# Later four modulation rows read transposed by DMA, with one VectorE product and sum per 128 columns

## Chip, cores and metric

The kernel runs on one core of a Trainium2 chip. The metric is the device time of one execution in microseconds, lower is better; before the change the three runs gave 842.69, 842.85 and 844.57 us, median 842.85 us. One further execution was profiled; every time inside a trace below is of that execution and is counted from its first instruction.

## What is computed

One transformer layer with adaptive layer norm: a condition vector `c` makes six rows of 1024 numbers, which scale and shift the inputs of two blocks and gate their outputs. The first block is linear attention, the second a SwiGLU feed-forward. Matrices are bf16, 2048 tokens, width 1024, feed-forward width 3584.

```python
mod = (_silu(c) @ w_mod).reshape(1, 6, 1, -1)          # c (1, 1024), w_mod (1024, 6*1024)
sa, ca, ga, sb, cb, gb = (mod[:, i] for i in range(6))
h = _layernorm(x) * (1 + ca) + sa
q, k, v = split(h @ wqkv)                              # 32 heads of 32
pq, pk = phi(q), phi(k)                                # phi(t) = where(t > 0, t + 1, exp(t)) + 1e-6
kv, z = pk^T v, sum(pk)                                # per head
o = (pq kv) / (pq z + 1e-6)
x = x + ga * (o @ wo)
h = _layernorm(x) * (1 + cb) + sb
x = x + gb * ((silu(h @ w_gate) * (h @ w_up)) @ w_down)
```

The change concerns how four of the six rows, `ga`, `cb`, `sb` and `gb`, are made from `w_mod`. Rows `sb` and `cb` are needed with their 1024 numbers down the 128 partitions (eight columns of 128, tiles `sbT` and `cb1T`), because they are per-partition operands of a modulation; rows `ga` and `gb` are needed on every partition, 1024 numbers along it (`ga_bc`, `gb_bc`), because they scale the columns of `wo` and `w_down`.

## The kernel before

The tokens are four blocks of 512 (`sc` 0 to 3), each of four tiles of 128 (`st`). The width is eight chunks of 128 columns (`cc`), the contraction of every projection. A projection group is eight matmuls of 128x512, 1.73 us on TensorE.

The schedule is written out by hand. `add(label, fn)` builds a list of groups: V(0,0..7), then for each block KV(sc), Q(0,..) once, K(sc+1,0..7), V(sc+1,0..7), then Q(1..3), then GU(sc,0..27) (gate and up columns of the feed-forward) and D (the down projection). `put(label, fn)` hangs work behind a group. What is put goes into the in-order queues of the engines at that place, so the label fixes the order on each engine, and nothing else does. K(2,3) below is the group of block 2, number 3, of the K projection.

- `k_group` and `q_group` (L255, L269) leave their result in one of five PSUM banks in rotation (`nextbank`, L237). A K or Q result is taken out by one ScalarE exponential (L244) and two VectorE instructions (L245, L246); a V result by one ScalarE copy (L267). A bank is written again five groups later, so an evacuation may be late by a few groups before TensorE waits.
- `ln` (L223) normalizes a token tile: statistics on VectorE (L203 to L207), small steps and the normalization on GpSimd (L209 to L218), then a DMA transpose from the SP queue (L227) that lays the tile into `M4` with its columns down the partitions. Block 2 is normalized while K(1,..) runs, block 3 while K(2,..) runs. `modulate` (L231, eight VectorE instructions for each block, put at V(1,4), V(1,6) and V(2,4), V(2,6)) must be done before the first K group of that block reads `M4`.
- `nd_tr` (L473) and `o_tr` (L504) are DMA transposes from the ScalarE queue, used in Q(1..3) and in GU(0,2) to GU(0,24). `o_mm` (L485) is the output projection of one token tile, 16 matmuls, put into GU(0,..) too.
- `load_x` (L140), the weight loads (L516, L517), the loads of `w_mod` and of `wo` (L620) are issued from the SP queue in order.

The four late rows before the change: `load_late` (L299) loads half a row's columns, 1 MB, with `w_mod`'s rows down the partitions (eight rows on each partition, `j`). For `cb`, TensorE multiplies these with `silu(c)` as 64 matmuls of one column (`late_vec`, L328, at K(1,2) and K(1,6)). For `ga`, `sb` and `gb`, VectorE sums the eight rows of each partition with their factors, 512 columns at a time (`late_sum`, L305 and L307), and splits the sum into a bf16 part and a bf16 rest (`late_split`, L312, L313); a matmul with ones then adds over the partitions, spread over all of them for `ga` and `gb` (`late_bc`, L342, then a ScalarE copy L343) or as columns for `sb` (`late_cols`, L320). `ga` is used when `wo` is scaled (L637, eight VectorE instructions), `gb` when `w_down` is (L683).

Of the kernel before, what the change touches and what calls it, by code (L numbers as in the profile page):

```python
# [21 lines left out]
def kernel(  # L22
# [19 lines left out]
    DC = D // P  # L42
# [20 lines left out]
    wo_v = A_wo.rearrange("(c p) n -> p c n", p=P)  # L63
# [13 lines left out]
    bank = [psum.tile([P, NB], F32, name=f"bank{i}") for i in range(8)]  # L77
# [3 lines left out]
    M3 = const.tile([P, 16384], BF16, name="M3")  # L81
    M4 = const.tile([P, NSC, DC, SCW], BF16, name="M4")
    M5 = const.tile([P, 14336], BF16, name="M5")
    M6 = const.tile([P, 8192], BF16, name="M6")
    M7 = const.tile([P, 12288], BF16, name="M7")

    def view(region, off, shape, dtype=BF16):
        n = 1
        for s_ in shape:
            n *= s_  # L90
        w = n * (2 if dtype == F32 else 1)
        ap = region[:, off:off + w]
        if dtype == F32:
            ap = ap.bitcast(F32)
        if len(shape) == 2:
            ap = ap.rearrange("p (a b) -> p a b", a=shape[0])
        elif len(shape) == 3:
            ap = ap.rearrange("p (a b c) -> p a b c", a=shape[0], b=shape[1])
        return ap
# [5 lines left out]
    wd_lo = view(M12, 14336, [14, D])  # L105
    wme = view(M3, 0, [DC, 2 * D])
    pqT = view(M3, 0, [NSC, HG, SCW])
    wml = [view(M3, 4096 * (1 + i), [DC, NB]) for i in range(3)]
    wd_hi = view(M3, 0, [14, D])
    pk = view(M5, 0, [STC, D])  # L110
    v_c = view(M5, 4096, [STC, HG, VW])
# [6 lines left out]
    wo = view(M6, 0, [DC, D])  # L118
    x1rs = [view(M6, 2048 * i, [D], F32) for i in range(2)]
    obs = [view(M6, 4096 + 1024 * i, [D]) for i in range(2)]  # L120
    accA = view(M5, 8256, [D], F32)
    hlA = [view(M5, 10304 + 1024 * i, [2, NB]) for i in range(2)]
    accG = view(M3, 12288, [D], F32)
    hlG = view(M3, 14336, [2, NB])
    xs = [view(M7, 1024 * i, [D]) for i in range(6)]
    xns = [view(M7, 6144 + 1024 * i, [D]) for i in range(6)]
    wgs = [view(M7, 4096 * i, [DC, FBW]) for i in range(3)]
# [41 lines left out]
    ident = const.tile([P, P], BF16, name="ident")  # L169
# [8 lines left out]
    sbT = const.tile([P, DC], BF16, name="sbT")  # L178
    cb1T = const.tile([P, DC], BF16, name="cb1T")
    m1 = const.tile([P, 6, DC], BF16, name="m1")  # L180
    ga_bc = const.tile([P, D], BF16, name="ga_bc")
    gb_bc = const.tile([P, D], BF16, name="gb_bc")
    KVZ = const.tile([P, HG, KVW], BF16, name="KVZ")
    ones = const.tile([P, P], BF16, name="ones")
    nc.gpsimd.memset(ones[:], 1.0)
    scF = const.tile([P, DC], F32, name="scF")

    scT = const.tile([P, DC], BF16, name="scT")
    nc.scalar.activation(out=scT[:], in_=c_sb[:], func=ACT.Silu)
    nc.scalar.copy(out=scF[:], in_=scT[:])  # L190

    def warm(n):
        for _ in range(n):
# [100 lines left out]

    GA, SB, CB, GB = 2, 3, 4, 5

    def load_late(q, kb, slot):
        k0 = q * D + kb * NB
        nc.sync.dma_start(out=wml[slot], in_=wm_v[:, :, k0:k0 + NB])  # L299

    def late_sum(acc, kb, slot, js):
        dst = acc[:, kb * NB:(kb + 1) * NB]
        for j in js:
            if j == 0:
                nc.vector.tensor_scalar_mul(out=dst, in0=wml[slot][:, 0, :], scalar1=scF[:, 0:1])  # L305
            else:
                nc.vector.scalar_tensor_tensor(out=dst, in0=wml[slot][:, j, :], scalar=scF[:, j:j + 1], in1=dst,  # L307
                                         op0=ALU.mult, op1=ALU.add)

    def late_split(acc, kb, hl):  # L310
        src = acc[:, kb * NB:(kb + 1) * NB]
        nc.vector.tensor_copy(out=hl[:, 0, :], in_=src)  # L312
        nc.vector.tensor_tensor(out=hl[:, 1, :], in0=src, in1=hl[:, 0, :], op=ALU.subtract)  # L313

    def late_cols(q, kb, hl):
        o = 320 + 8 * q
        for ii in range(NB // P):
            col = o + kb * (NB // P) + ii
            for s_ in range(2):
                nc.tensor.matmul(bank[7][:, col:col + 1], lhsT=hl[:, s_, ii * P:(ii + 1) * P], rhs=ones[:, 0:1],  # L320
                                 start=False, stop=(s_ == 1), skip_group_check=True)

    def late_vec(q, kb, slot):
        o = 320 + 8 * q
        for ii in range(NB // P):
            col = o + kb * (NB // P) + ii
            for j in range(DC):
                nc.tensor.matmul(bank[7][:, col:col + 1], lhsT=wml[slot][:, j, ii * P:(ii + 1) * P],  # L328
                                 rhs=scT[:, j:j + 1], start=False, stop=(j == DC - 1), skip_group_check=True)

    def late_fin(q):
        mps = bank[7][:, 320 + 8 * q:328 + 8 * q]
        if q == SB:
            nc.vector.tensor_copy(out=sbT[:], in_=mps)
        else:
            nc.vector.tensor_copy(out=m1[:, q, :], in_=mps)
            nc.vector.tensor_scalar_add(out=cb1T[:], in0=m1[:, q, :], scalar1=1.0)

    def late_bc(kb, hl, dst):
        b = nextbank()  # L340
        for s_ in range(2):
            nc.tensor.matmul(b[:], lhsT=ones[:], rhs=hl[:, s_, :], start=(s_ == 0), stop=(s_ == 1))  # L342
        nc.scalar.copy(out=dst[:, kb * NB:(kb + 1) * NB], in_=b[:])  # L343


    def tr0(st):
# [101 lines left out]
    def put(label, *fns):  # L448
        after.setdefault(label, []).extend(fns)
# [156 lines left out]
    put(("V", 1, 7), lambda: [load_x(st) for st in range(12, 16)])  # L606


    def sums(acc, kb, slot, labels):
        for i, lab in enumerate(labels):  # L610
            put(lab, lambda i=i: late_sum(acc, kb, slot, (2 * i, 2 * i + 1)))

    put(("V", 0, 6), lambda: load_late(CB, 0, 0), lambda: load_late(CB, 1, 1), lambda: load_late(GA, 0, 2))
    put(("K", 1, 2), lambda: late_vec(CB, 0, 0), lambda: load_late(GA, 1, 0))
    put(("K", 1, 6), lambda: late_vec(CB, 1, 1), lambda: load_late(SB, 0, 1))
    put(("V", 1, 7), lambda: late_fin(CB))
    sums(accA, 0, 2, [("V", 1, k) for k in range(4)])
    put(("V", 1, 3), lambda: late_split(accA, 0, hlA[0]), lambda: load_late(SB, 1, 2))
    put(("K", 2, 2), lambda: late_bc(0, hlA[0], ga_bc))
    put(("K", 2, 3), lambda: nc.sync.dma_start(out=wo, in_=wo_v))  # L620
    sums(accA, 1, 0, [("V", 2, k) for k in range(4)])
    put(("V", 2, 3), lambda: late_split(accA, 1, hlA[1]))
    put(("K", 3, 0), lambda: late_bc(1, hlA[1], ga_bc))
    for kb in range(2):
        sums(accA, kb, 1 + kb, [("V", 3, 4 * kb + k) for k in range(4)])
    put(("V", 3, 4), lambda: late_split(accA, 0, hlA[0]))
    put(("KV", 3, 0), lambda: late_split(accA, 1, hlA[1]))
    put(("Q", 1, 2), lambda: late_cols(SB, 0, hlA[0]), lambda: late_cols(SB, 1, hlA[1]), lambda: late_fin(SB))
    put(("GU", 0, 18), lambda: load_late(GB, 0, 0), lambda: load_late(GB, 1, 1))
    gb_at = [("GU", 0, f) for f in range(21, FC)] + [("GU", 1, f) for f in range(8)]  # L630
    for kb in range(2):
        sums(accG, kb, kb, gb_at[5 * kb:5 * kb + 4])
        put(gb_at[5 * kb + 3], lambda kb=kb: late_split(accG, kb, hlG))
        put(gb_at[5 * kb + 5], lambda kb=kb: late_bc(kb, hlG, gb_bc))
    for cc in range(DC):
        put(("K", 3, 2 + cc) if cc < 6 else ("V", 3, cc - 6),
            lambda cc=cc: nc.vector.tensor_tensor(out=wo[:, cc, :], in0=wo[:, cc, :], in1=ga_bc[:], op=ALU.mult))  # L637


    put(("KV", 3, 1), kvz_build)  # L640
# [82 lines left out]
```

## Time and profile before

| | |
|---|---|
| median of three runs | 842.85 us |
| profiled execution, whole time | 842.25 us |
| its span, first to last instruction | 840.4 us |
| TensorE clock granted | 0.999 |
| one projection group (8 matmuls, TensorE) | 1.73 us |
| K(1,0) to K(1,7) start | 60.71 us |
| V(1,0) start | 76.12 us |
| K(2,0) start | 90.84 us |
| V(2,0) start | 106.00 us |
| K(3,0) start | 120.72 us |
| GU(0,18) start | 307.70 us |

The whole time is 1.85 us more than the span: what lies before the first and after the last instruction. A stage of the kernel is read from the chain of waits, which lists TensorE's groups by start; a stage's load on the other engines is read from the timeline of each engine in that stretch. A group's `idle before` names what the engine waited for last. Busy shares over the whole span hide that VectorE is nearly full from 66 to 92 us and from 97 to 122 us and lightly used after 370 us.

### The profile page before, as it was taken

What the parts mean: (1) busy time and instruction counts of PE and PEld (TensorE: products, weight loads), DVE (VectorE), ACT (ScalarE), POOL (GpSimd) and SP (SyncE); (2) the same over time, 40 slices, a digit from 0 to 9 for tenths busy, and PEclk for the clock granted to TensorE, in tenths of its full rate; (3) what the DMA queues carried; (4) which work ended last, traced back from release to release, by engine and by line L of the source; (5) the groups of instructions that cost most, each with busy time, mean ns of one, the idle gap of its engine ahead of it and who ended that gap; (6) DMA issues with size and microseconds to landing.
All of it is one profiled execution on the core that took longest, in us unless ns stands there. A gap on an engine that the chain in (4) does not pass through costs nothing.

```text
span 840.4 us, 10723 instructions
## 1 busy us (share of the span) xinstructions
PE 833.5 (99%) x4292; PEld 391.3 (47%) x4292; DVE 356.5 (42%) x668; ACT 145.1 (17%) x271; POOL 79.9 (10%) x143
## 2 busy tenths in 40 slices
PE   8999999999999999999999999999999999999998
PEld 4454444544444444444444444444444444444445
DVE  5768779988655656635341111111101211111111
ACT  4333333323211111111110001111000111100000
POOL 2124220022122323100000000000000000000000
PEclk9999999999999999999999999999999999999999
DMA  9985491056599899787874225555322555211210
GB/s 291 310 244 138 133 243 46 16 154 133 126 225 225 224 226 287 190 248 226 251 241 142 76 69 151 151 151 152 105 75 82 156 155 152 76 38 44 76 69 26
DMA packets 203905, 128.62 MB, mean 153 GB/s; under 512 B 50768, under 2 KB 190032, under 8 KB 203856
## 3 DMA queue, kind: packets, MB, share of 16 engines
q1 hardware_dynamic: 163008, 98.58, 41.1%
q10 hardware_dynamic: 38544, 20.98, 11.4%
q0 software_dynamic: 2304, 8.39, 2.6%
q8 instruction: 33, 0.54, 0.3%
q14 instruction: 16, 0.13, 0.1%
HBM read 103.81 MB, written 12.58 MB: 139 GB/s over the span
## 4 chain that ended last, share of the span: by engine, by line
PE 97%; SPq 1%; DMA 1%; issue 0%; DVE 0%
PE bank L553 23%; PE bank L534 23%; PE bank L528 23%; PE bank L272 7%; PE bank L485 7%; PE bank L264 7%; PE bank L249 6%; DMA M<-in_w_mod_dram 1%; PE bank L458 1%; PE bank L281 1%; SPq L148 1%; SPq L145 0%; PE bank L342 0%; SPq L140 0%; PE bank L328 0%; PE bank L364 0%
## 5 line engine op out<-in xcount | busy, mean ns | idle before, releaser
L534 PE MATMUL bank<-M,M 128*128 128x512 bf16 x896 | 211.7, 379 | 0.0
L528 PE MATMUL bank<-M,M 128*128 128x512 bf16 x896 | 211.6, 379 | 0.0
L536 DVE TENSOR_TENSOR M<-bank,e 128x512 bf16<-128x512 f32 x112 | 77.5, 692 | 248.5 <-PE bank L534 247.1
L553 PE MATMUL bank<-M,M 128*128 128x512 bf16 (+2 forms) x728 | 148.0, 363 | 0.0
L531 ACT ACTIVATE e<-bank 128x512 f32<-128x512 f32 x112 | 66.8, 597 | 436.3 <-PE bank L528 423.6
L553 PEld LDWEIGHTS <-M 128*128 128x128 bf16 x952 | 90.9, 98 | 103.0
L534 PEld LDWEIGHTS <-M 128*128 128x128 bf16 x896 | 87.7, 98 | 105.7
L528 PEld LDWEIGHTS <-M 128*128 128x128 bf16 x896 | 87.3, 98 | 103.9
L556 DVE TENSOR_TENSOR M<-bank,M 128x512 bf16<-128x512 f32 (+2 forms) x34 | 22.5, 661 | 169.9 <-PE bank L553 169.9
L249 PE MATMUL bank<-M,M 128*128 128x512 bf16 x256 | 57.9, 379 | 1.0 <-DVE M L231 0.6
L485 PE MATMUL bank<-M,M 128*128 128x512 bf16 x256 | 57.9, 379 | 0.0
L272 PE MATMUL bank<-M,M 128*128 128x512 bf16 x256 | 57.7, 379 | 0.0
L264 PE MATMUL bank<-M,M 128*128 128x512 bf16 x256 | 55.9, 379 | 0.0
L244 ACT ACTIVATE e<-bank 128x512 f32<-128x512 f32 x64 | 37.8, 598 | 100.5 <-PE bank L272 48.8
L553 PE MATMUL bank<-M 128*128 128x512 bf16 x224 | 51.0, 379 | 0.0
L246 DVE SCALAR_TENSOR_TENSOR M<-bank,e 128x512 bf16<-128x512 f32 x64 | 44.3, 692 | 3.9
L264 PEld LDWEIGHTS <-M 128*128 128x128 bf16 x256 | 25.0, 98 | 30.2
L485 PEld LDWEIGHTS <-M 128*128 128x128 bf16 x256 | 25.0, 98 | 29.7
L249 PEld LDWEIGHTS <-M 128*128 128x128 bf16 x256 | 24.2, 98 | 29.5 <-DVE M L231 2.1
L245 DVE TENSOR_SCALAR e<-e 128x512 f32<-128x512 f32 x64 | 27.7, 433 | 23.4 <-ACT e L244 23.4
L272 PEld LDWEIGHTS <-M 128*128 128x128 bf16 x256 | 24.5, 98 | 27.6
L487 DVE TENSOR_TENSOR M<-bank,M 128x512 f32<-128x512 f32 x32 | 22.0, 689 | 13.3 <-PE bank L485 13.1
(74 smaller groups left out, 362.4 us busy)
## 6 DMA issues: line engine op xcount, KB each, us to landing
M<-in_B_w_gate_dram SPq DMA_DIRECT2D x56, 512.0 KB, 3.9
M<-in_B_w_up_dram SPq DMA_DIRECT2D x56, 512.0 KB, 4.9
M<-in_w_mod_dram SPq DMA_DIRECT2D x8, 1024.0 KB, 8.7
x_scratch<-M POOLq DMA_DIRECT2D x16, 512.0 KB, 5.6
M<-x_scratch ACTq DMA_DIRECT2D x16, 512.0 KB, 3.4
M<-in_B_w_down_dram SPq DMA_DIRECT2D x6, 1024.0 KB, 7.9
M<-in_A_x_dram SPq DMA_DIRECT2D x16, 256.0 KB, 6.6
M<-in_w_mod_dram SPq DMA_DIRECT2D x8, 512.0 KB, 7.1
```

The lines of the kernel that those rows point to most:

```text
L244: nc.scalar.activation(out=e[:], in_=acc, func=ACT.Exp)
L245: nc.vector.tensor_scalar(out=e[:], in0=e[:], scalar1=1.0, scalar2=PHI_EPS, op0=ALU.min, op1=ALU.add)
L246: nc.vector.scalar_tensor_tensor(out=dst, in0=acc, scalar=0.0, in1=e[:], op0=ALU.max, op1=ALU.add)
L249: nc.tensor.matmul(acc[:], lhsT=M4[:, sc_, cc, t * P:(t + 1) * P], rhs=wk[:, cc, h * NB:(h + 1) * NB], start=(cc == 0), stop=(cc == DC - 1))
L264: nc.tensor.matmul(acc[:], lhsT=M4[:, sc_, cc, t * P:(t + 1) * P], rhs=wv[:, cc, h * NB:(h + 1) * NB], start=(cc == 0), stop=(cc == DC - 1))
L272: nc.tensor.matmul(acc[:], lhsT=wq[:, cc, qc * P:(qc + 1) * P], rhs=M4[:, sc_, cc, :], start=(cc == 0), stop=(cc == DC - 1))
L485: nc.tensor.matmul(acc[:], lhsT=oTs[st % 3][:, cc, :], rhs=wo[:, cc, hs], start=(cc == 0), stop=(cc == DC - 1))
L528: nc.tensor.matmul(g_ps[:], lhsT=wg_blk[:, cc, fs], rhs=M4[:, sc_, cc, :], start=(cc == 0), stop=(cc == DC - 1))
L531: nc.scalar.activation(out=sg[:], in_=g_ps[:], func=ACT.Silu)
L534: nc.tensor.matmul(u_ps[:], lhsT=wu_blk[:, cc, fs], rhs=M4[:, sc_, cc, :], start=(cc == 0), stop=(cc == DC - 1))
L536: nc.vector.tensor_tensor(out=gus[sc_][:, f, :], in0=u_ps[:], in1=sg[:], op=ALU.mult)
L553: nc.tensor.matmul(y_ps[:, 0:w], lhsT=gus[sc_][:, f, t * P:(t + 1) * P], rhs=wd(f)[:, c0:c1], start=(f == 0), stop=(f == FC - 1))
```

## The change

All four late rows are now made alike. A row's 1024x1024 piece of `w_mod` is read by eight DMA transposes of 128x1024 each (source in HBM), so that the columns of `w_mod` lie down the partitions and its 1024 rows along them (`rowT`). `silu(c)` is spread over all partitions once (`sc_bc`). For each 128 columns one VectorE instruction then multiplies 1024 elements with `sc_bc` and sums them into one number per partition (`colF`). That is already the column form that `cb` and `sb` need. For `ga` and `gb` the column is repeated 128 times along the partition (`spread` into `rep`) and eight TensorE transposes of 128 columns turn it into the spread row (`late_bc`). `late_vec`, `late_split` and `late_cols` are gone, `gb_bc` shares the storage of `ga_bc`, and `rowT[1]` lies where `wo` will be, so that the load of `wo` moves from K(2,3) to V(2,5) and the scaling of `wo` from K(3,2)..V(3,1) to K(3,0)..K(3,7).

```diff
-    wml = [view(M3, 4096 * (1 + i), [DC, NB]) for i in range(3)]
-    accA = view(M5, 8256, [D], F32)
-    hlA = [view(M5, 10304 + 1024 * i, [2, NB]) for i in range(2)]
-    accG = view(M3, 12288, [D], F32)
-    hlG = view(M3, 14336, [2, NB])
+    rowT = [view(M3, 4096, [DC, DC, P]), view(M6, 0, [DC, DC, P])]
+    prod = [view(M5, 8256, [D], F32), view(M3, 12288, [D], F32)]
...
-    gb_bc = const.tile([P, D], BF16, name="gb_bc")
+    gb_bc = ga_bc
...
+    rep = const.tile([P, DC, P], BF16, name="rep")
+    sc_bc = const.tile([P, D], BF16, name="sc_bc")
+    colF = const.tile([P, 6, DC], F32, name="colF")
...
+    def load_late(q, i, js):
         for j in js:
+            nc.sync.dma_start_transpose(out=rowT[i][:, j], in_=wm_v[:, j, q * D:(q + 1) * D])
+
+    def late_sum(q, i, pr, bs):
+        for b in bs:
+            nc.vector.tensor_tensor_reduce(out=prod[pr].rearrange("p (j k) -> p j k", j=DC), in0=rowT[i][:, :, b, :],
+                                           in1=sc_bc[:].rearrange("p (j k) -> p j k", j=DC), scale=1.0, scalar=0.0,
+                                           op0=ALU.mult, op1=ALU.add, accum_out=colF[:, q, b:b + 1])
+
+    def late_fin(q):
+        if q == SB:
+            nc.vector.tensor_copy(out=sbT[:], in_=colF[:, q, :])
+        else:
+            nc.vector.tensor_copy(out=m1[:, q, :], in_=colF[:, q, :])
+            if q == CB:
+                nc.vector.tensor_scalar_add(out=cb1T[:], in0=m1[:, q, :], scalar1=1.0)
             else:
+                spread(nc.vector, m1[:, q, :])
+
+    def spread(eng, col):
+        eng.tensor_copy(out=rep[:], in_=col.unsqueeze(2).to_broadcast([P, DC, P]))
+
+    def late_bc(dst):
+        tp = nextbank()[:].bitcast(BF16).rearrange("p (c s) -> p c s", c=DC)
+        for cc in range(DC):
+            nc.tensor.transpose(tp[:, cc, :], rep[:, cc, :], ident[:])
+        nc.scalar.copy(out=dst[:].rearrange("p (c s) -> p c s", c=DC), in_=tp)
...
-    put(("V", 0, 6), lambda: load_late(CB, 0, 0), lambda: load_late(CB, 1, 1), lambda: load_late(GA, 0, 2))
-    put(("K", 1, 2), lambda: late_vec(CB, 0, 0), lambda: load_late(GA, 1, 0))
-    put(("K", 1, 6), lambda: late_vec(CB, 1, 1), lambda: load_late(SB, 0, 1))
-    put(("V", 1, 7), lambda: late_fin(CB))
-    sums(accA, 0, 2, [("V", 1, k) for k in range(4)])
-    put(("V", 1, 3), lambda: late_split(accA, 0, hlA[0]), lambda: load_late(SB, 1, 2))
-    put(("K", 2, 2), lambda: late_bc(0, hlA[0], ga_bc))
-    put(("K", 2, 3), lambda: nc.sync.dma_start(out=wo, in_=wo_v))
-    sums(accA, 1, 0, [("V", 2, k) for k in range(4)])
-    put(("V", 2, 3), lambda: late_split(accA, 1, hlA[1]))
-    put(("K", 3, 0), lambda: late_bc(1, hlA[1], ga_bc))
...
+    put(("V", 0, 1), lambda: spread(nc.gpsimd, scT[:]))
+    put(("V", 0, 5), lambda: late_bc(sc_bc))
+
+    def put_late(q, i, loads, sums, pr=0):
+        n = DC // len(loads)
+        for k, lab in enumerate(loads):
+            put(lab, lambda k=k: load_late(q, i, range(n * k, n * (k + 1))))
+        for k, lab in enumerate(sums):
+            put(lab, lambda k=k: late_sum(q, i, pr, (2 * k, 2 * k + 1)))
+        put(sums[-1], lambda: late_fin(q))
+
+    put_late(GA, 0, [("V", 0, 7), ("Q", 0, 2)], [("V", 1, k) for k in range(4)])
+    put(("K", 2, 2), lambda: late_bc(ga_bc))
+    put_late(CB, 1, [("Q", 0, 4), ("Q", 0, 6)], [("V", 2, k) for k in range(4)])
+    put(("V", 2, 5), lambda: nc.sync.dma_start(out=wo, in_=wo_v))
+    put_late(SB, 0, [("V", 1, 4), ("V", 1, 5), ("V", 1, 6), ("V", 1, 7)], [("V", 3, k) for k in range(4)])
+    put_late(GB, 0, [("GU", 0, 18 + k) for k in range(4)], [("GU", 0, 23 + k) for k in range(4)], 1)
+    put(("GU", 1, 0), lambda: late_bc(gb_bc))
     for cc in range(DC):
-        put(("K", 3, 2 + cc) if cc < 6 else ("V", 3, cc - 6),
-            lambda cc=cc: nc.vector.tensor_tensor(out=wo[:, cc, :], in0=wo[:, cc, :], in1=ga_bc[:], op=ALU.mult))
+        put(("K", 3, cc), lambda cc=cc: nc.vector.tensor_tensor(out=wo[:, cc, :], in0=wo[:, cc, :], in1=ga_bc[:],
+                                                               op=ALU.mult))
```

In the built program of the changed kernel each product and sum is two VectorE instructions, the product over 1024 elements and a read of the accumulator (128x1), and each product waits for the accumulator read before it. A DMA transpose from the SP queue and one from the ScalarE queue wait for each other's landing wherever they are neighbours in the order.

More of the change, by code (lines that the diff above doesn't have):

```diff
@@ L181 @@
     ga_bc = const.tile([P, D], BF16, name="ga_bc")
-    gb_bc = const.tile([P, D], BF16, name="gb_bc")
+    gb_bc = ga_bc
     KVZ = const.tile([P, HG, KVW], BF16, name="KVZ")
-    ones = const.tile([P, P], BF16, name="ones")
-    nc.gpsimd.memset(ones[:], 1.0)
-    scF = const.tile([P, DC], F32, name="scF")
+    rep = const.tile([P, DC, P], BF16, name="rep")
+    sc_bc = const.tile([P, D], BF16, name="sc_bc")
+    colF = const.tile([P, 6, DC], F32, name="colF")
     scT = const.tile([P, DC], BF16, name="scT")
     nc.scalar.activation(out=scT[:], in_=c_sb[:], func=ACT.Silu)
-    nc.scalar.copy(out=scF[:], in_=scT[:])
     def warm(n):
@@ L295 @@
     GA, SB, CB, GB = 2, 3, 4, 5
[L297 to L302, printed above, removed]
-        for j in js:
-            if j == 0:
-                nc.vector.tensor_scalar_mul(out=dst, in0=wml[slot][:, 0, :], scalar1=scF[:, 0:1])
-            else:
-                nc.vector.scalar_tensor_tensor(out=dst, in0=wml[slot][:, j, :], scalar=scF[:, j:j + 1], in1=dst,
-                                         op0=ALU.mult, op1=ALU.add)
@@ L310, in late_split @@
[L310 to L343, printed above, removed]
+    def load_late(q, i, js):
+        for j in js:
+            nc.sync.dma_start_transpose(out=rowT[i][:, j], in_=wm_v[:, j, q * D:(q + 1) * D])
[4 more added lines that the diff above has]
+                                           op0=ALU.mult, op1=ALU.add, accum_out=colF[:, q, b:b + 1])
@@ L606 @@
     put(("V", 1, 7), lambda: [load_x(st) for st in range(12, 16)])
-    def sums(acc, kb, slot, labels):
-        for i, lab in enumerate(labels):
-            put(lab, lambda i=i: late_sum(acc, kb, slot, (2 * i, 2 * i + 1)))
-    put(("V", 0, 6), lambda: load_late(CB, 0, 0), lambda: load_late(CB, 1, 1), lambda: load_late(GA, 0, 2))
-    put(("K", 1, 2), lambda: late_vec(CB, 0, 0), lambda: load_late(GA, 1, 0))
-    put(("K", 1, 6), lambda: late_vec(CB, 1, 1), lambda: load_late(SB, 0, 1))
-    put(("V", 1, 7), lambda: late_fin(CB))
@@ L617 @@
-    sums(accA, 0, 2, [("V", 1, k) for k in range(4)])
-    put(("V", 1, 3), lambda: late_split(accA, 0, hlA[0]), lambda: load_late(SB, 1, 2))
-    put(("K", 2, 2), lambda: late_bc(0, hlA[0], ga_bc))
-    put(("K", 2, 3), lambda: nc.sync.dma_start(out=wo, in_=wo_v))
-    sums(accA, 1, 0, [("V", 2, k) for k in range(4)])
-    put(("V", 2, 3), lambda: late_split(accA, 1, hlA[1]))
-    put(("K", 3, 0), lambda: late_bc(1, hlA[1], ga_bc))
-    for kb in range(2):
-        sums(accA, kb, 1 + kb, [("V", 3, 4 * kb + k) for k in range(4)])
@@ L626 @@
[L626 to L634, printed above, removed]
+    put(("V", 0, 1), lambda: spread(nc.gpsimd, scT[:]))
```

## The prediction

> **What bounds the kernel now.** I read the page first, then the chain of waits, then VectorE's timeline around the starts of K(2,0) and K(3,0), and the SP and ScalarE queues in GU(0,16) to GU(0,24).
>
> ```profile
> PE 833.5 (99%) x4292; PEld 391.3 (47%) x4292; DVE 356.5 (42%) x668; ACT 145.1 (17%) x271; POOL 79.9 (10%) x143
> ...
> PE 97%; SPq 1%; DMA 1%; issue 0%; DVE 0%
> ...
> 65.89 0.78 PE bank L328 x32
> ...
> 73.59 0.78 PE bank L328 x32
> ...
> 96.93 0.43 PE bank L342 x2
> ...
> 156.68 0.38 PE bank L320 x16
> ```
>
> From 28 us on TensorE never waits: the chain is its groups end to end. So only two things change the time: instructions taken from or given to TensorE, and new waits on it. The four lower lines price the first.
>
> ```profile
> 79.75 0.15 DVE L207 TENSOR_SCALAR veps<-mv 128x1 f32<-128x1 f32 x1
> 79.82 0.48 DVE L305 TENSOR_SCALAR M<-M,scF 128x512 f32<-128x512 bf16 x1
> 80.33 6.30 DVE L307 SCALAR_TENSOR_TENSOR M<-M,scF,M 128x512 f32<-128x512 bf16 x7
> ...
> 87.73 2.67 DVE L231 TENSOR_SCALAR M<-M,ca1T,saT 128x512 bf16<-128x512 bf16 x8
> ...
> 110.50 0.15 DVE L207 TENSOR_SCALAR veps<-mv 128x1 f32<-128x1 f32 x1
> ...
> 118.86 2.67 DVE L231 TENSOR_SCALAR M<-M,ca1T,saT 128x512 bf16<-128x512 bf16 x8 [0.29 <-DMA M<-M]
> ```
>
> VectorE is full before K(2,0) and K(3,0). The modulation of block 2 ends at 90.40, K(2,0) starts at 90.84 and reads its eighth chunk 7 x 0.216 us later, at 92.3: 1.9 us to spare. For block 3 it is 121.5 against 122.2: 0.7 us. What makes VectorE later there makes TensorE later.
>
> ```profile
> 299.25 2.12 ACTq L473 DMA_TRANSPOSE M<-M  x1
> ...
> 302.10 3.59 ACTq L504 DMA_TRANSPOSE M<-M  x1
> 305.79 0.60 ACT L531 ACTIVATE e<-bank 128x512 f32<-128x512 f32 x1 [6.33 <-PE bank L528]
> ...
> 310.07 1.63 ACTq L473 DMA_TRANSPOSE M<-M  x1
> ...
> 312.50 3.73 ACTq L504 DMA_TRANSPOSE M<-M  x1
> 316.59 0.60 ACT L531 ACTIVATE e<-bank 128x512 f32<-128x512 f32 x1 [6.31 <-PE bank L528]
> ```
>
> In GU(0,..) ScalarE's queue carries transposes between the activations that free the banks. A transpose that waits holds up the activation behind it.
>
> [...]692 ns for L246, 512 elements[...]L307 repeats every 0.90 us in V1 beside GpSimd's normalization, every 0.78 us in V3 without[...]
>
> **TensorE's own work.** Removed: 2 x 0.78 (L328), four pairs of L342 at 0.43, and 0.38: 3.67 us. Added: 3 x 8 transposes. Short matmuls L281 run 16 in 0.91 us, 57 ns each, so eight cost 0.45 and all 1.36. Net -2.3 us, the whole possible gain, and about the 0.3% (2.5 us) below which no change can be told.
>
> **sc_bc at V(0,5).** GpSimd's spread stands behind the first normalization, which ends at 41.42. At L218's 1.19 us it ends at 42.6; TensorE finishes V(0,5) at 31.27 + 6 x 1.727 = 41.63. It waits 1.0 us (between 0 and 1.6: repeated input unknown). The next transposes of block 1 come 1.2 us later; the modulation at 53.8 hides that.
>
> **Stage V1.** One new sum: 1.22 for the product, and an accumulator read near the 0.15 us of a 128x1 instruction less overlap, with a wait for the result: 1.35 (bounds 1.2 and 1.5). Eight are 10.8, plus 0.7 to 0.85 beside GpSimd (the 7 x 0.12 of L307): 11.5 us. The old sums and split took 79.82 to 87.73, 7.9. Then `late_fin` adds 0.2 and the spread on VectorE, repeated input[...], 1.2. VectorE enters V1 at 79.8 + 1.0 + 0.45 - 0.2 (a gap of L328's that closes) = 81.1. Sums end 92.6, modulation runs 94.0 to 96.6, K(2,0) ends 96.9. Unhindered it would end at 92.57 + 1.45 - 1.56 = 92.46. **Loss 4.4 us** (2.5 to 5.5).
>
> **Stage V2.** Count from K(2,0)'s end T. VectorE's K2 work ended at T + 18.0 before (110.57 against 92.57). Now the loads of x tiles 12 to 15 stand on SP behind six of the eight `sb` transposes, which wait for the last `ga` sum (92.6). Six issues are 7.5 us, the load lands some 3.5 us later, at 104; VectorE wants it at T + 4.5 = 101.4, so it waits 2.5. K2 work ends at T + 20.5 = 117.4, the `cb` sums at 128.9, modulation at 132.0, K(3,0) at 132.3. TensorE would be there at T + 28.15 + 1.73 = 126.8. **Loss 5.5 us** (2 if the x load is in time, 10 if transposes from HBM are slower). Other stages let this pass: five banks cover K2.
>
> **wo.** Its load waits for the last `cb` sum (128.9) and lands 10.2 us on (as before), 139.7 with issue. VectorE stands at the first scaling until then, and K(3,1)'s bank is free at 141.4; TensorE wants it at 132.3 + 0.9 + 5 x 1.73 = 141.8. Hidden by 0.4; each us later costs one. Afterwards scaling and evacuation repeat every 1.73 us (129.64, 131.37 before), TensorE's pace. `sb` sums end near Q(1,0)'s evacuation as before: nothing.
>
> **GB in GU(0,18) to GU(1,1).** The order is: SP pair, `nd_tr(15)`, SP pair, `o_tr(12)`, SP pair, `o_tr(13)`, SP pair, `o_tr(14)`, each waiting for the landing before it. A transpose there landed 4.8 to 7.4 us after issue (at 288.4 and 299.25), against 3.1 in quiet stretches. With 6.1 for a pair and 4.8 for a single: 308.5, 314.6, 319.4, 325.5. ScalarE then stands at `o_tr(12)` until 325.5 with GU(0,19)'s activation behind it, done 327.6; the fifth bank group after it wanted to start at 323.2: 4.5 us. The last pair lands near 347, the sums (8 x 1.35 with evacuations between) and the spread end at 364, and `late_bc` at GU(1,0) wants it at 361: 3.5 us more. With 4.5 and 3.2 all of this is hidden; at 7 and 5 it is about 13. I take **7 us** (0 to 13).
>
> Sum: 1.45 - 1.56 + 4.4 + 5.5 - 1.2 (L342 and L320 less the last two spreads) + 7 = 15.6. On the profiled execution, 842.25 (span 840.4 and 1.85 around it), 857.8; the median shown is 0.6 higher, so **858.4**.
>
> **Rivals.**
> 1. Only VectorE's stages cost, the alternation of queues doesn't: landings of 3 us. For it: quiet stretches show 3.1. Against: those in GU(0,16) to GU(0,20) show 6 to 12. 858.4 - 7 = 851.4; with the x load in time, 848.
> 2. HBM-sourced transposes occupy the queue far longer. At 3 us each, sixteen last from 52 to 100 instead of 73, block 2's four transposes follow to 105, landing 108: V1 loses 14 rather than 4.4, V2 4 more, GB 10 more, 882. It decides from about 2 us each (block 2 late at 92). For it: pieces of 256 bytes from HBM appear nowhere in the trace of before. Against: L227's 1.25[...].
> 3. Not slower: the new sum is cheap. VectorE must start modulating by 89.5 to hold nothing up; from 81.1, less 1.4 for fin and spread, 7.0 us are left for eight: 0.88 each. If it took [...] (0.69 as L683, 1024 elements), with GB landing fast and the x load in time, only -2.3 + 1.0 remains: 841.5. Against: the output is f32, and L307, f32 out, takes 748 for 512.
>
> **How the numbers follow.** Forecast 0.52 (850 to 868); rival 1 0.24 (845 to 852); rival 2 0.15 (866 to 895); rival 3 0.09 (839.5 to 845.3). The range 846 to 870 holds the forecast, nearly all of rival 1 and the low end of rival 2, and leaves out about 0.2. Slower (over 845.4): 0.91. Same, most of rival 3: 0.06. Faster would need no wait at all: 0.03.
>
> **What would show it.** L299 products near 1.2 us with a short read after each; K(2,0)'s and K(3,0)'s matmuls waiting for VectorE L227 of the new file (modulation), about 4 us each; VectorE waiting for an x load near 101 us; ScalarE idle ahead of `o_tr(12)` for a w_mod transpose, and TensorE gaps near 330 and 370 us; SP's w_mod transposes 1.3 us apart. I am wrong if the sums take under 0.9 us, or if TensorE shows gaps elsewhere, above all in K3 (wo).

## The result, and the profile after it

The changed kernel took 861.95 us (median of five runs, 860.67 to 864.75) against 842.69 us for the kernel before (five runs, 842.46 to 844.57): a ratio of 1.0228, 95% interval 1.0206 to 1.0250, so 2.3% slower. The profiled execution took 861.95 us too; its span is 860.1 us, 19.7 us above the span of before. What follows explains these 19.7 us. One execution among all those below, the one of run 2 that was profiled (885.37 us), ran from start to end at a lower granted clock (0.946); it is left out of that run's time, and its trace is read only for which waits it holds. Line numbers are now those of the changed kernel: L299 is the new product and sum, L295 its DMA transposes, L227 the modulation, L245 the K groups, L314 and L319 the spread and its TensorE transposes, L462 the output projection, L505 and L511 gate and up, L508 their activation, L481 `o_tr`, L450 `nd_tr`, L600 the load of `wo`, L605 its scaling.

First the page's busy line and its chain, as before, then TensorE's own list of waits (what it stood for, us in total, times, longest; the lines left out are waits before V(0,0)).

```profile
PE 832.0 (97%) x4148; PEld 390.6 (45%) x4228; DVE 357.2 (42%) x676; ACT 145.4 (17%) x269; POOL 83.1 (10%) x143
...
PE 86%; DVE 7%; DMA 2%; SPq 2%; issue 1%; POOL 0%; ACT 0%; ACTq 0%; DVEq 0%; POOLq 0%
```

```profile
PE bank L245 <- DVE M L227: 7.7, 4, 4.2
PE bank L462 <- ACT e L508: 5.8, 1, 5.8
PE bank L245 <- DVE M L242: 1.7, 1, 1.7
...
PE bank L319 <- POOL rep L314: 0.8, 1, 0.8
```

VectorE is busy as long as before (357.2 against 356.5 us): the change has not given it more work, it has put the work elsewhere. The chain, 97% TensorE before, is 86% now. Four kinds of wait carry the loss: the modulations (L227) ahead of K(2,0) and K(3,0), ScalarE's activation (L508) in front of an output projection, a bank in K2 (L242), and GpSimd's spread.

Where each was lost is read by comparing when the same TensorE group starts in the two traces (TensorE's timeline, which counts some starts 0.1 to 0.2 us earlier than the chain that the table of before was read from; us):

| start of | before | changed | difference |
|---|---|---|---|
| V(0,0) | 31.10 | 31.56 | +0.46 |
| K(1,0) | 60.54 | 62.44 | +1.90 |
| V(1,0) | 75.96 | 76.25 | +0.29 |
| K(2,1) | 93.31 | 97.99 | +4.68 |
| V(2,0) | 105.83 | 112.40 | +6.57 |
| K(3,1) | 123.62 | 135.69 | +12.07 |
| GU(0,18) | 307.70 | 319.26 | +11.56 |
| GU(0,22) | 328.42 | 348.48 | +20.06 |
| GU(1,8) | 381.08 | 400.73 | +19.65 |
| first down group | 450.14 | 469.80 | +19.66 |

So, as differences of neighbouring lines, 4.4 us go in stage V1 with K(2,0), 1.9 in K2, 5.5 in V2 with K(3,0), 8.5 between GU(0,18) and GU(0,22). V0 adds 1.4 with the spread of `silu(c)`, and K1 gives 1.6 back (the matmuls of `late_vec` are gone). Between K(3,1) and GU(0,18) 0.5 us come back and behind GU(0,22) 0.4, mostly because the old matmuls L320 and L342 are gone there. From GU(1,8) on nothing changes.

VectorE's timeline ahead of K(2,0) (start, duration, what) is to be held against the one of before; the third product, at 84.30, is the only slow one of the eight.

```profile
81.76 1.22 DVE L299 CUSTOM_DVE_ANT_0 M<-M,sc_bc 128x1024 f32<-128x1024 bf16 x1 [0.26 <-issue]
82.91 0.08 DVE L299 DVE_READ_ACCUMULATOR2_ANT colF<- 128x1 f32 x1
...
84.30 2.10 DVE L299 CUSTOM_DVE_ANT_0 M<-M,sc_bc 128x1024 f32<-128x1024 bf16 x1
...
91.50 1.22 DVE L299 CUSTOM_DVE_ANT_0 M<-M,sc_bc 128x1024 f32<-128x1024 bf16 x1
...
92.97 0.69 DVE L314 COPY rep<-m 128x1024 bf16<-128x1024 bf16 x1
93.58 2.67 DVE L227 TENSOR_SCALAR M<-M,ca1T,saT 128x512 bf16<-128x512 bf16 x8
```

A product lasts 1.22 us, its read 0.08, and the next starts 1.27 after it. Eight, one of them slow, last from 81.76 to 92.73; the modulation that began at 87.73 before begins at 93.58. TensorE's timeline shows the consequence, here and one block later; the first two lines are of before, the others of the changed kernel:

```profile
90.68 1.89 PE L249 MATMUL bank<-M,M 128*128 128x512 bf16 x8
...
120.55 1.89 PE L249 MATMUL bank<-M,M 128*128 128x512 bf16 x8
```

```profile
94.05 3.20 PE L245 MATMUL bank<-M,M 128*128 128x512 bf16 x8 [2.91 <-DVE M L227]
97.08 1.07 PE L277 MATMUL bank<-M 128*128 128x129 bf16 x16
...
131.45 3.27 PE L245 MATMUL bank<-M,M 128*128 128x512 bf16 x8 [4.17 <-DVE M L227]
134.56 1.07 PE L277 MATMUL bank<-M 128*128 128x129 bf16 x16
```

From the start of these eight matmuls to the start of what follows it is 3.03 us here and 3.11 one block later, instead of 1.73. Two things slow them. They follow their chunks of the modulation, 0.33 us apart; where only that holds them the group takes 2.49 (K(3,0) in run 3 below, from 127.34 to 129.83; the K matmuls behind it go at 0.22 us each, as in a group of 1.73). The rest, 0.5 us, is the clock: 0.50 granted from 94 to 96 us, 0.66 over the 4 us from 94 on.

In K2 the queue of SP and VectorE (timeline) show the loads of x tiles 12 to 15 (L137) behind six `sb` transposes, which wait for the last `ga` sum, and VectorE waiting for the first of them (the first line is of before, where L140 is the same load):

```profile
87.25 2.95 SPq L140 DMA_DIRECT2D M<-in_A_x_dram  x4
```

```profile
92.76 8.91 SPq L295 DMA_TRANSPOSE M<-in_w_mod_dram  x6
101.73 1.99 SPq L137 DMA_DIRECT2D M<-in_A_x_dram  x4
```

```profile
105.98 1.29 DVE L199 BATCH_NORM_STATS2 stats<-M 128x6 f32<-128x512 bf16 x2 [4.21 <-DMA M<-in_A_x_dram]
...
119.58 1.23 DVE L299 CUSTOM_DVE_ANT_0 M<-M,sc_bc 128x1024 f32<-128x1024 bf16 x1
...
130.98 2.67 DVE L227 TENSOR_SCALAR M<-M,ca1T,saT 128x512 bf16<-128x512 bf16 x8
```

From 105.98 to the end of this modulation VectorE's timeline has no wait. So the start of K(3,0) is set by when the x load landed and by VectorE's work behind it. TensorE's wait of 1.7 us for a bank in K2 is a part of the same lateness: without it TensorE would have waited that much longer ahead of K(3,0).

And the feed-forward stage, timeline of all engines:

```profile
319.53 16.73 SPq L295 DMA_TRANSPOSE M<-in_w_mod_dram  x4
...
330.42 1.25 ACTq L450 DMA_TRANSPOSE M<-M  x1
...
333.07 1.89 PE L462 MATMUL bank<-M,M 128*128 128x512 bf16 x8
...
338.81 1.25 ACTq L481 DMA_TRANSPOSE M<-M  x1
340.16 0.60 ACT L508 ACTIVATE e<-bank 128x512 f32<-128x512 f32 x1 [18.32 <-DMA M<-in_B_w_gate_dram]
...
340.81 3.57 PE L462 MATMUL bank<-M,M 128*128 128x512 bf16 x8 [5.85 <-ACT e L508]
...
344.18 2.74 PE L505 MATMUL bank<-M,M 128*128 128x512 bf16 x8
...
346.76 1.89 PE L511 MATMUL bank<-M,M 128*128 128x512 bf16 x8
```

In the kernel before, the same output projection runs without a gap:

```profile
321.51 3.62 PE L485 MATMUL bank<-M,M 128*128 128x512 bf16 x16
```

The first pair of `gb` transposes is issued at 319.53 and 322.80 and lands 10.1 and 7.5 us later; `nd_tr(15)` starts at 330.42, when both are in; the second pair starts at 333.59, when that is in; `o_tr(12)` starts at 338.81, when the pair is in. The releaser that the profile names for the activation is a weight load; the two issued at 317.26 and 318.99 had landed after 3.7 and 5.6 us, so it wasn't that: the instruction ahead of it in ScalarE's queue is what held it. TensorE ran out of banks at 334.96 and stood 5.85 us. The eight matmuls after the wait then take 3.37 us to the start of the next group and the gate group behind them 2.58, instead of 1.73 each: in that stretch, 340.8 to 346.5 us, the granted clock is 0.55. So the wait cost 8.5 us, not 5.9. By the microsecond the granted clock is 0.50 in each from 340.8 to 345.8, and 1.00 from 346.7 on. The shorter wait of 2.91 us ahead of K(2,0) had 0.50 behind it too, for 2 us.

### The profile page after: what moved, and what is told of

It is laid out like the page before. It is cut to its first block, busy times and chain, and to the rows that moved or that the text cites. A ratio compares the mean times of both kernels' runs of the same rounds, so it can differ in the third digit from the quotient of the medians.

```text
span 860.1 us, 10559 instructions
## 1 busy us (share of the span) xinstructions
PE 832.0 (97%) x4148; PEld 390.6 (45%) x4228; DVE 357.2 (42%) x676; ACT 145.4 (17%) x269; POOL 83.1 (10%) x143
## 4 chain that ended last, share of the span: by engine, by line
PE 86%; DVE 7%; DMA 2%; SPq 2%; issue 1%; POOL 0%; ACT 0%; ACTq 0%; DVEq 0%; POOLq 0%
PE bank L530 22%; PE bank L505 22%; PE bank L511 22%; PE bank L462 6%; PE bank L268 6%; PE bank L245 3%; DVE M L299 2%; PE bank L260 2%; DVE M L242 2%; DVE stats L199 1%; DMA M<-in_A_x_dram 1%; DMA M<-in_w_mod_dram 1%; PE bank L435 1%; DVE e L241 1%; SPq L295 1%
## 5 line engine op out<-in xcount | busy, mean ns | idle before, releaser
L505 PE MATMUL bank<-M,M 128*128 128x512 bf16 x871 | 210.5, 380 | 1.3
L511 PE MATMUL bank<-M,M 128*128 128x512 bf16 x880 | 210.3, 379 | 0.9
L508 ACT ACTIVATE e<-bank 128x512 f32<-128x512 f32 x112 | 66.5, 597 | 446.3 <-PE bank L505 395.7
L511 PEld LDWEIGHTS <-M 128*128 128x128 bf16 x896 | 87.7, 98 | 105.7
L505 PEld LDWEIGHTS <-M 128*128 128x128 bf16 x896 | 87.5, 98 | 104.6 <-issue 1.7
L245 PE MATMUL bank<-M,M 128*128 128x512 bf16 x247 | 59.6, 392 | 10.4 <-DVE M L227 7.7
L462 PE MATMUL bank<-M,M 128*128 128x512 bf16 x254 | 59.6, 387 | 6.0 <-ACT e L508 5.8
L242 DVE SCALAR_TENSOR_TENSOR M<-bank,e 128x512 bf16<-128x512 f32 x64 | 44.3, 692 | 3.9
L245 PEld LDWEIGHTS <-M 128*128 128x128 bf16 x256 | 24.8, 99 | 41.3 <-DVE M L227 13.2
L462 PEld LDWEIGHTS <-M 128*128 128x128 bf16 x256 | 25.3, 99 | 36.7 <-issue 7.8
L299 DVE CUSTOM_DVE_ANT_0 M<-M,sc_bc 128x1024 f32<-128x1024 bf16 x32 | 40.9, 1278 | 1.1 <-issue 0.3
```

The lines of the kernel that those rows point to most:

```text
L242: nc.vector.scalar_tensor_tensor(out=dst, in0=acc, scalar=0.0, in1=e[:], op0=ALU.max, op1=ALU.add)
L245: nc.tensor.matmul(acc[:], lhsT=M4[:, sc_, cc, t * P:(t + 1) * P], rhs=wk[:, cc, h * NB:(h + 1) * NB], start=(cc == 0), stop=(cc == DC - 1))
L299: nc.vector.tensor_tensor_reduce(out=prod[pr].rearrange("p (j k) -> p j k", j=DC), in0=rowT[i][:, :, b, :], in1=sc_bc[:].rearrange("p (j k ...
L462: nc.tensor.matmul(acc[:], lhsT=oTs[st % 3][:, cc, :], rhs=wo[:, cc, hs], start=(cc == 0), stop=(cc == DC - 1))
L505: nc.tensor.matmul(g_ps[:], lhsT=wg_blk[:, cc, fs], rhs=M4[:, sc_, cc, :], start=(cc == 0), stop=(cc == DC - 1))
L508: nc.scalar.activation(out=sg[:], in_=g_ps[:], func=ACT.Silu)
```

## Experiments

Each kernel is the changed kernel but for the edit shown. Theory A is that the time is lost in the waits named above; the rivals are in the expectations.

**1. The `gb` row later.**

```diff
-put_late(GB, 0, [("GU", 0, 18 + k) for k in range(4)], [("GU", 0, 23 + k) for k in range(4)], 1)
-put(("GU", 1, 0), lambda: late_bc(gb_bc))
+put_late(GB, 0, [("GU", 0, 25), ("GU", 0, 26)], [("GU", 1, k) for k in range(4)], 1)
+put(("GU", 1, 5), lambda: late_bc(gb_bc))
```

> The gb row's eight transposes are issued at GU(0,25) and GU(0,26), after the last transpose of ScalarE's queue, its sums at GU(1,0) to GU(1,3), its spread row at GU(1,5). Theory A (the gb transposes and ScalarE's transposes wait for each other's landing, ScalarE stands at o_tr(12), the banks run out): TensorE's wait of 5.8 us at 335 to 341 us and the 2.6 us of slow matmuls behind it go, 862.0 - 8.4 = 853.5 us (852 to 855). Rival B (what costs there is the bytes on the DMA engines and the eight sums on VectorE, wherever they stand): the wait shows up again at GU(1,..), 860 us or more.

861.86 us (860.62 to 862.81), ratio to the kernel before 1.0225 (1.0204 to 1.0247): a miss for A's number. The wait at GU(0,20) is gone (the difference to before stays at 11.15 us from GU(0,18) to GU(0,26)), but 8.4 us come back between GU(0,27) and GU(1,6). Timeline of SP and ScalarE in this run:

```profile
350.68 16.07 SPq L295 DMA_TRANSPOSE M<-in_w_mod_dram  x3
...
361.05 1.25 ACTq L481 DMA_TRANSPOSE M<-M  x1
362.40 1.57 ACT L508 ACTIVATE e<-bank 128x512 f32<-128x512 f32 x3 [9.96 <-PE bank L505]
```

SP issued its first transpose ahead of `o_tr(15)`; it landed after 10.3 us, and ScalarE stood until 361.05 with three activations behind it. The next weight loads stood behind the other transposes on SP (TensorE waits 1.6 us for one), and VectorE, standing at the first sum for 11 us, held up the products that free the banks (2.9 us). Three waits in place of one: the label had been moved, the mutual waiting had not been removed. B's number came out, but the run doesn't say whether bytes or waiting made it; the next bears on that.

**2. The same bytes, not transposed.**

```diff
+if q == GB:
+    nc.sync.dma_start(out=rowT[i][:, j], in_=wm_v[:, j, q * D:(q + 1) * D].rearrange("p (c s) -> p c s", c=DC))
+else:
     nc.sync.dma_start_transpose(...)
```

> At the same places as in the changed kernel the gb row's eight pieces of 256 KB are loaded as they lie in HBM instead of transposed (so gb itself is not computed); same bytes, same queue, same eight sums. Theory A (mutual waiting of transposes): no stall at o_tr(12), 853.5 us (852 to 855.5). Rival B (bytes and VectorE work): nothing or at most 2 us come back, 860 us or more.

853.59 us (three executions, 852.57 to 856.97), ratio to the kernel before 1.0136 (1.0106 to 1.0166): A's number. This kernel leaves `gb` out: what it sums is not the row. TensorE's list of waits no longer has ScalarE's activation in it. The same 2 MB on the same queue, followed by the same sums, did not bring the stall back, so B is out. The edit takes two things away at once, though: the waiting of transposes on two queues for one another, and the transposing itself, which could load the DMA engines more than a plain read of the same bytes. Run 6, which keeps the transposes and puts them on one queue, bears on that.

**3. x loads ahead of `sb`'s transposes.**

```diff
-put_late(SB, 0, [("V", 1, 4), ("V", 1, 5), ("V", 1, 6), ("V", 1, 7)], [("V", 3, k) for k in range(4)])
+put_late(SB, 0, [("V", 2, k) for k in range(4)], [("V", 3, k) for k in range(4)])
```

> The sb row's eight transposes are issued at V(2,0) to V(2,3) instead of V(1,4) to V(1,7), so that the loads of x tiles 12 to 15 no longer stand behind six of them. Theory A: VectorE's wait of 4.2 us for an x load at 101.8 us goes; with it the 1.7 us bank wait in K2, and VectorE comes to the cb sums 4.2 us earlier, TensorE 1.7 us earlier, so that of the 5.5 us lost ahead of K(3,0) some 2.5 go too: 4.2 us in all, 857.8 us (856.5 to 859.5). Rival C (the eight cb sums alone set K(3,0), the x load is hidden): at most 1 us, 861 us or more.

867.23 us (864.86 to 867.71), 5 us slower than the changed kernel; neither number. (The profiled execution is the fastest of the four; it is 2.9 us slower than the changed kernel's.) The wait for the x load is gone and K(3,0) starts 127.34 instead of 131.45, 4.1 us earlier, but from K(3,1) to V(3,0) it loses 7.9 us against the kernel before (timeline):

```profile
133.53 0.53 SPq L600 DMA_DIRECT2D M<-in_A_wo_dram  x1
143.36 0.69 DVE L605 TENSOR_TENSOR M<-M,ga_bc 128x1024 bf16<-128x1024 bf16 x1 [11.48 <-DMA M<-in_A_wo_dram]
...
145.24 4.43 PE L245 MATMUL bank<-M,M 128*128 128x512 bf16 x10 [5.70 <-DVE M L242]
```

The load of `wo` now stood behind the transposes on SP, VectorE stood at the first scaling for 11.5 us with the evacuations of K3 behind it, and the banks ran out. That is the step called "hidden by 0.4" in the prediction, with its price seen.

**4. The same with `wo` ahead of the transposes too.** The first line is the changed kernel's.

```diff
-put_late(SB, 0, [("V", 1, 4), ("V", 1, 5), ("V", 1, 6), ("V", 1, 7)], [("V", 3, k) for k in range(4)])
+put_late(SB, 0, [("V", 2, 6), ("V", 2, 7), ("K", 3, 0), ("K", 3, 1)], [("V", 3, k) for k in range(4)])
```

> As the run with the x loads first, but sb's transposes stand behind the load of wo too (V(2,6), V(2,7), K(3,0), K(3,1)). In the run with the x loads first TensorE came to K(3,0) 4.1 us earlier against the changed kernel and then lost 5.7 us and more in K3, where VectorE stood 11.5 us at the first scaling of wo, whose load had been issued 133.5 us behind the eight sb transposes instead of 130.6. Theory A (the x load behind sb's transposes costs 4 to 5 us, and wo's lateness took it back): with wo in time again 862.0 - 4.5 = 857.5 us (856.5 to 859). Rival C (the cb sums alone set K(3,0) and what follows): 861 us or more.

859.75 us, but from 855.0 to 862.7 in four executions, more than the effect, so the time settles nothing. Read from the stage: between KV(1), which stands behind V1, and Q(1,0) the changed kernel loses 11.55 us against before (runs 1 and 6, which leave this stage alone, 11.7 and 11.9), this one 8.85. VectorE waits for `wo` 3.7 us and TensorE doesn't. So the x loads cost 2.7 us where they stood, between the two theories' numbers: without that wait the `cb` sums set K(3,0) all the same, with 1.7 us of waiting, the pace of the modulation and slow matmuls behind it: the sixteen short ones of L277 at 132.07 take 2.17 us to the start of the next group, at 160.06 us they take 0.91.

**5. Fewer sums in the full stages.** Six in V1, six in V2, four in K3, eight in V3; `sb`'s loads, the load of `wo` and its scaling follow.

```diff
-put_late(GA, 0, [...], [("V", 1, k) for k in range(4)])
-put(("K", 2, 2), lambda: late_bc(ga_bc))
-put_late(CB, 1, [...], [("V", 2, k) for k in range(4)])
-put(("V", 2, 5), lambda: nc.sync.dma_start(out=wo, in_=wo_v))
-put_late(SB, 0, [("V", 1, 4), ("V", 1, 5), ("V", 1, 6), ("V", 1, 7)], [("V", 3, k) for k in range(4)])
+put_late(GA, 0, [...], [("V", 1, 0), ("V", 1, 1), ("V", 1, 2), ("V", 2, 0)])
+put(("K", 3, 0), lambda: late_bc(ga_bc))
+put_late(CB, 1, [...], [("V", 2, 1), ("V", 2, 2), ("K", 3, 1), ("K", 3, 2)])
+put(("K", 3, 3), lambda: nc.sync.dma_start(out=wo, in_=wo_v))
+put_late(SB, 0, [("V", 2, 3 + k) for k in range(4)], [("V", 3, k) for k in range(4)])
...
-    put(("K", 3, cc), lambda cc=cc: nc.vector.tensor_tensor(out=wo[:, cc, :], ...))
+    put(("V", 3, 4 + cc // 2), lambda cc=cc: nc.vector.tensor_tensor(out=wo[:, cc, :], ...))
```

> Six of the 24 sums in V1 (ga), six in V2 (two of ga, four of cb), four of cb at K(3,1) and K(3,2), the eight of sb in V3; sb's transposes, wo's load and its scaling follow them. VectorE's sums take the time that the old ones took in each stage (6 x 1.27 = 7.6 us against 7.9). Theory A (VectorE late for the two modulations, and the x load): all of 4.2 + 1.7 + 5.5 us goes, 850.5 us (849 to 852.5). Rival D (VectorE has no room, the delay only moves to K3, V3 and Q1): more than 5 us of it come back there, 856 us or more.

855.21 us (853.99 to 856.34), ratio 1.0145 (1.0127 to 1.0164). By GU(0,18) TensorE is 1.66 us behind the kernel before, against 11.56: 9.9 of the 11.4 us are back. K(2,0) is on time; K(3,0) still waits 1.1 us. A's number was missed all the same: the profiled execution, 854.56 us, is 4.1 us over 850.5. Of these, 1.5 are what is left of the 11.4, and 2.5 are in the stall at GU(0,20), which the edit leaves alone and which is 11.0 us in this trace (8.5 in the changed kernel, 8.0 and 10.5 in runs 3 and 4). Its size follows how late the first pair lands: less each run's own lateness at GU(0,18), `nd_tr(15)` starts at 318.9 in the changed kernel and 319.1 in run 3, at 320.5 in run 4 and 320.8 here. D falls: in K3 and V3 VectorE has the room. The edit moves sums, loads and the scaling together; what each is worth alone it doesn't say.

**6. The `gb` transposes on ScalarE's queue**, two each at GU(0,25), (0,26), (0,27), GU(1,0), sums at GU(1,3..6), `late_bc` at GU(1,7):

```diff
-nc.sync.dma_start_transpose(out=rowT[i][:, j], ...)
+(nc.scalar if q == GB else nc.sync).dma_start_transpose(out=rowT[i][:, j], ...)
```

> The gb row's eight transposes are issued from ScalarE's own queue, two each at GU(0,25), (0,26), (0,27) and GU(1,0), behind the last o_tr, so that no transpose of another queue has to land first; sums at GU(1,3) to GU(1,6), spread row at GU(1,7). Theory A (what costs is the wait for the landing of the other queue's transposes, with activations behind it on ScalarE; moved to GU(0,25) on SP it came back because one gb transpose still went ahead of o_tr(15), because weight loads stood behind gb transposes on SP, and because the sums stood on VectorE before their data came): all 8.4 us go, 853.5 us (852.5 to 855). Rival B' (the transposes slow the feed-forward's loads wherever they stand, or eight issues on ScalarE hold up the activations): half or more stays, 857.5 us or more.

856.51 us (855.02 to 862.16), between the two. The stall is gone: the difference to before is 11.26 us at GU(0,18) and 10.40 at GU(1,7). Run 1 had the same transposes at almost the same groups on SP, and ScalarE stood for one of them; here they are on ScalarE's own queue and it stands no more. With run 2 this leaves the mutual waiting of the two queues as the cause of the stall. (The sums stand three groups later than in run 1, so not all of the difference between the two runs is the queue's.) Behind GU(1,7) 2.3 us are lost: the last sum and the spread end at about the moment at which TensorE wants the eight transposes, and it waits 1.7 us for them.

**7 and 8. All remedies, then the spread row later.** Sums 6, 4, 6, 8 in V1, V2, K3, V3; `sc_bc` at Q(0,5); `gb` as in run 6. Run 8 moves `late_bc(gb_bc)` from GU(1,7) to GU(1,9) and starts the scaling of `w_down` three groups later. Against runs 5 and 6:

```diff
-put(("V", 0, 5), lambda: late_bc(sc_bc))
+put(("Q", 0, 5), lambda: late_bc(sc_bc))
-put_late(CB, 1, [...], [("V", 2, 1), ("V", 2, 2), ("K", 3, 1), ("K", 3, 2)])
+put_late(CB, 1, [...], [("V", 2, 1), ("K", 3, 1), ("K", 3, 2), ("K", 3, 3)])
...
-put(("GU", 1, 7), lambda: late_bc(gb_bc))
+put(("GU", 1, 9), lambda: late_bc(gb_bc))
-    put(("GU", 1, max(3 * i + 4, 7 + i) + k // 2) ...)
+    put(("GU", 1, max(3 * i + 4, 7 + i) + 3 + k // 2) ...)
```

> All remedies at once: sums 6 in V1, 4 in V2, 6 in K3, 8 in V3 with the x loads ahead of sb's transposes, sc_bc's transposes at Q(0,5), the gb row on ScalarE's queue as in the run beside it. Theory A (the change costs only by its waits, TensorE's own work is 2.3 us less): no wait of TensorE is left, 842.5 - 2.0 = 840.5 us (839.5 to 841.5), below the kernel before. Rival E (a stage is full on VectorE or on the DMA engines whatever the order): 843.5 us or more.

> As the run with all remedies, but the spread row of gb is made at GU(1,9) instead of GU(1,7) and the scaling of w_down starts three groups later, because VectorE's last gb sum and spread ended at 383.5 us where TensorE wanted the eight transposes at 381. Theory A: the 4.2 us between GU(1,7) and GU(1,9) go, 843.0 us (842 to 844). Rival: the scaling, later by three groups, is late for the down projection or holds up the evacuations, 845 us or more.

Run 7: 847.18 us, ratio 1.0054 (1.0039 to 1.0068), 4.6 us of it lost behind GU(1,7), as in run 6 (2.3 in the wait, 0.5 for the eight transposes themselves, the rest in slow matmuls behind them). Run 8: 843.17 us against 842.41 us, ratio 1.0011 (1.0004 to 1.0017). A's number for run 8 holds. A's for run 7 doesn't, and the rival E of run 7 is right in part: the kernel never gets below the one before. The waits that are left on TensorE in run 8 behind V(0,0):

```profile
...
PE bank L260 <- DVE M L242: 0.9, 1, 0.9
PE bank L245 <- DVE M L227: 0.6, 2, 0.4
...
PE bank L435 <- DVE M L444: 0.2, 1, 0.2
```

At V(2,0) run 8 is 1.45 us ahead of the kernel before, at GU(0,18) 1.20 us behind: between them VectorE is nearly full (busy 42.9 of the 45 us from 130 to 175), and the sums that V1 and V2 no longer hold press on K(3,0), V(3,0) and Q1. So nearly all of the 19.7 us were waits that an order can avoid. That the saving on TensorE is used up by VectorE having no slack is read from these waits and that busy time; no run shows it by an edit, since run 9, meant to, met something else.

**9. `wo` scaled on GpSimd**, otherwise run 8.

```diff
-    put(("V", 3, 4 + cc // 2), lambda cc=cc: nc.vector.tensor_tensor(out=wo[:, cc, :], ...))
+    put(("V", 3, 4 + cc // 2), lambda cc=cc: nc.gpsimd.tensor_tensor(out=wo[:, cc, :], ...))
```

> The same, and the eight scalings of wo (4.9 us of VectorE at 151 to 156 us, behind the sb sums) are computed on GpSimd, which is idle there. If VectorE's fullness from K3 to Q(2,..) is what still costs (0.9 us ahead of V(3,0), 0.8 and 0.5 us in Q1 and Q2), the last two go: 841.7 us (840.8 to 843). If GpSimd contends with VectorE or is too slow for o_mm(0) at Q(2,1), it is no faster than the run beside it.

850.99 us, 8 us slower than run 8: the expected 841.7 is missed, and the rival, that GpSimd contends with VectorE, holds. Timelines of VectorE and GpSimd:

```profile
144.04 1.22 DVE L299 CUSTOM_DVE_ANT_0 M<-M,sc_bc 128x1024 f32<-128x1024 bf16 x1
...
145.31 3.07 DVE L299 CUSTOM_DVE_ANT_0 M<-M,sc_bc 128x1024 f32<-128x1024 bf16 x1
...
148.42 3.02 DVE L299 CUSTOM_DVE_ANT_0 M<-M,sc_bc 128x1024 f32<-128x1024 bf16 x1
```

```profile
145.17 21.84 POOL L605 TENSOR_TENSOR M<-M,ga_bc 128x1024 bf16<-128x1024 bf16 x8 [29.78 <-DMA M<-in_A_wo_dram]
```

From 145.17 on, while GpSimd multiplies two operands from SBUF, VectorE's product goes from 1.22 to 3.02 us; five of them lose 9 us, and the first `nd` group waits 5.0 us for VectorE.

## Why the prediction held

The forecast, 858.4 us, was 3.6 us under the median; the causes it names are the ones the runs show, and its sum of 15.6 us stands against 19.7. That it came so near is in part luck, since several sizes were off in opposite directions. By its steps:

- **TensorE's own work.** Right: K1 gives 1.6 us back where L328 stood, V0 takes 0.45 for eight transposes, and eight matmuls of L319 last that long in all three places.
- **`sc_bc` at V(0,5).** 1.0 forecast, 0.82 measured. GpSimd's spread took 1.04, not 1.19 us. Run 7 removes it.
- **Stage V1.** 4.4 forecast, 4.4 measured. That the number is exact is luck, the parts were off and cancelled: the product lasts the 1.22 us that the author had estimated (no trace of before shows one of 1024 elements with f32 output), but a sum repeats every 1.27, not 1.35, and the spread on VectorE takes 0.69, not 1.2 (an estimate too), so that the modulation began at 93.58 and not at 94.0, although VectorE came to the sums at 81.76 and not at 81.1; but the slow clock behind the wait, some 0.5 us, was not in the sum. One product beside GpSimd's normalization lost 0.88 (forecast 0.7 to 0.85). Run 5 shows the cause: with six sums K(2,0) is on time.
- **Stage V2 and K2.** 5.5 forecast, 7.4 measured (1.9 in K2, 5.5 at K(3,0)). The term that was too small is VectorE's wait for the x load. It was taken as 2.5 us, with the load landing at 104; it was 4.21, to 105.98, because the six transposes took 8.9 us to issue, not 7.5 (1.25 each, as L227 in the trace of before), and the load landed 4.25 us after its issue, not 3.5. The slow clock at K(3,0), 0.50 from 131 to 134 us, adds 0.6 that was not in the sum, and the quicker sums take 0.5 off. "Five banks cover K2" was wrong too: VectorE was so late that TensorE stood 1.7 us for a bank. That moved a part of the loss from K(3,0) to K2; it isn't on top of it. Run 4 puts the x load's share at 2.7 us.
- **`wo`.** Right: landed at 140.1 (139.7 forecast), no wait of TensorE. That it was hidden by very little is shown by run 3, where its load was issued 2.9 us later and TensorE came 4.1 us earlier: 7.9 us lost.
- **The `gb` row.** 7 forecast, 8.5 measured. The cause and its order are those forecast: in the changed kernel's own time, 11.56 us later, the forecast has ScalarE released at 337.1 and TensorE stopping at 334.8; the trace has 338.8 and 334.96. Two sizes failed. The term of 4.5 us for the wait was 5.85: the first pair took 10.9 us, to 330.42, and not 6.1, while `nd_tr(15)` and the second pair took less than forecast (3.2 against 4.8 and 5.2 against 6.1). And the slow clock after it, 2.6 us, was not in the sum. The second part, 3.5 us at GU(1,0), did not come: the stall itself had made TensorE later, and the spread row was in time. So the 7 came near 8.5 by luck, one part left out and one that didn't come. Runs 2 and 6 show that waiting across the queues is the cause, run 1 that a later label alone isn't enough.
- **Start.** 0.46 us at V(0,0) belong to this execution (in runs 1 and 3 to 9 that group starts between 30.9 and 33.0 us); no step of the change touches it.

The rivals: the first (stages alone, 851.4) is excluded by the stall at GU(0,20), which runs 2 and 6 take away. The second (transposes from HBM at 3 us each) is excluded by sixteen of them issued in 24.1 us, with landings of 3.8 to 5.7 us. The third needed sums of 0.88 us; they repeat every 1.27.

## What to carry to other kernels

Before moving work to an engine that looks half idle, count it against the stage in which it must be done: here the engine's total stayed the same, and 9.9 us (run 5) hung on which stage held which sums and loads. In this program a DMA transpose costs its landing to the next transpose of the other queue, and to all that stands behind that one on its engine (`nd_tr(15)` of the changed kernel started at 330.42, 10.9 us after the first of the pair ahead of it was issued): keep transposes of one stretch on one queue. When a wait of TensorE of several microseconds is forecast, add the slower matmuls behind it: 2.6 us behind 5.85 in the changed kernel, 1.7 behind 2.3 in run 7.

## What the runs showed of the hardware

- A product and sum over 1024 bf16 elements with f32 output repeats every 1.27 us (1.22 and a read of 0.08, partly beside the next). Beside GpSimd's one-operand normalization it lost 0.88 us once in V1 and once in V2, beside GpSimd's two-operand products 1.8 us each time.
- A copy on VectorE that repeats each input element 128 times, 1024 bf16 elements out, takes 0.69 us, as long as a product of two bf16 operands of that size (L605, 0.69); on GpSimd the copy takes 1.04 us.
- A DMA transpose from HBM, 256 KB, landed 3.5 us after issue at best, 3.8 to 5.7 for the sixteen issued in a row from 52.9 us on, and 10.1 and 10.3 us where it was issued within 2.5 us of two weight loads of 512 KB each.
- After a wait of 5.85 us TensorE's granted clock was 0.50 for 5 us and 0.55 over 5.7; after 2.91 us it was 0.50 for 2 us and 0.66 over 4. After the wait ahead of K(3,0) in run 3 the matmuls of K3 ran at 0.22 us each (39 in 8.58 us from 130.95 on); after 1.68 us of waiting at the same place in run 4 the sixteen of L277 took 2.17 us from 132.07 to the start of the next group, against 0.91 at 160.06.
